# Softmax division on ScalarE and GpSimd, its small constant stored beside the sums, and a schedule recomputed with shifts as users of the shared port

## The chip, the cores and the metric

The kernel runs on one core of one Trainium2 chip. The metric is the device time of one execution in microseconds; of several runs the median counts. A core has five engines that run side by side, each through its own list of instructions in order: TensorE (PE; its weight loads are shown apart as PEld), VectorE (DVE), ScalarE (ACT), GpSimd (POOL) and SyncE (SP), which here only issues DMAs.

## The reference

An attention over 4 batches, 8 heads, 768 positions and 64 dimensions, then a two-layer feed-forward with GELU on the 3072 x 512 result.

```python
scores = scale * np.matmul(q, k.transpose(0, 1, 3, 2))
keep = is_global | is_local              # 8 global columns, a causal window of 96
scores = scores + bias                   # -slope * distance, a slope for each head
scores = np.where(keep, scores, -1000000000.0)
scores = scores - np.max(scores, axis=-1, keepdims=True)
a = np.exp(scores)
a = a / (np.sum(a, axis=-1, keepdims=True) + 1e-09)
attn = np.matmul(a, v)
x = attn.transpose(0, 2, 1, 3).reshape(3072, 512)
h = x @ w_in                             # 512 -> 2048
g = 0.5 * h * (1.0 + erf(h / sqrt(2)))
out = g @ w_out                          # 2048 -> 512
```

The line that the change is about is the division `a / (sum + 1e-09)`.

## The kernel before, in words

The program has two parts. The first one does the attention, the first quarter of the feed-forward and the preparation of all weights. The second one does the other three quarters of the feed-forward by a scheme with fewer products (seven for eight), from weights that the first part wrote to memory.

First part: the tokens are cut into 12 chunks of 256 (three for each batch), and each chunk has 4 pairs of heads. Each piece of work is an operation with a letter, listed in `first_part`:

- `l` (SP) loads the queries, keys and values of one pair. `S` (PE, line 214) makes its scores, two banks of PSUM for each pair, one for each head. A head has two blocks of 128 rows; each is 256 columns wide, or one of them 128 in a batch's first chunk.
- `R` (DVE, line 231) adds the penalties, keeps the maximum (`nmax`) and writes the head's tile `pn`. `E` (ACT, line 244) takes the exponential in place, and its accumulator writes the row sum into `nsum`.
- `U` (DVE, lines 249 and 250) adds 1e-9 to the four sums of a pair and takes the reciprocal, both in place in `nsum`. There are 48 `U`.
- `N` (line 256) multiplies `pn` by the reciprocal, two instructions for each of the 96 heads, on DVE or on GpSimd.
- `T` (PE, line 266) transposes, `C` (ACT or DVE, through the helper `copy`, line 179) copies the result to SBUF as `pt`, and `A` (PE, line 287) multiplies by the values.
- `X` and `Y` split the result in a high and a low part, `W` (POOL, line 307) adds them up and `Z` writes them out. `m` (PE, lines 421 and 433), `G` (ACT, GELU), `K` (DVE, `gl`) and `n` (PE, line 457) are the feed-forward's first quarter, and `O` (ACT or DVE) copies its sums to the tile `o`.
- Weights arrive as 64-bit words. `D` (ACT line 322 or POOL line 320) scales the low word, `F` (DVE, line 327) shifts the high word, `j` (DVE, line 332) joins, `J` (POOL or DVE, line 337) adds the low bits. `H`, `L`, `Q`, `h`, `o` and `B` split, sum and store them (`wst`, `sums`).

The second part (from line 536 on) runs products `p` and `m2` on PE in a fixed order, with sums, GELUs and splits on DVE and ACT between.

The order on every engine is decided by `schedule`, which plays a list of costs through once while the program is built. An operation has one or several engines with a cost for each; it goes to the engine on which it would be done first, moved by a number from `BIAS`. Operations that the planner takes to use one port into SBUF, which DVE and GpSimd share, are marked `port=True`, and it lets no marked DVE operation overlap a GpSimd operation. Before the change `F` and `N` are not marked on DVE. `CAP` says how many PSUM banks a kind may hold (`ks` is for scores), and `DEC` gives due times for the weights' preparation. What the planner found is kept: each engine runs its instructions in that order and waits for what they need.

Of the kernel before, what the change touches and what calls it, by code (L numbers as in the profile page):

```python
# [64 lines left out]
def slope(h):  # L65
# [4 lines left out]
SUMS2 = {1: (0, 0), 2: (0, 1), 7: (1, 0), 5: (1, 1), 4: (2, 0), 3: (2, 1), 6: (3, 0)}  # L70
SLOTS = {"k": 8, "nat": 6, "pn": 10, "pt": 10, "x": 3, "xw": 1, "ws": 4, "wa": 4, "wst": 2, "sums": 1, "g": 3, "o": 2,
         "hc1": 2, "hc6": 2, "hc5": 2, "gb0": 5, "gb1": 7, "gx": 2}
CAP = {"ks": 4, "kt": 3, "ka": 2, "kh": 2, "ko": 2, "kb": 4}
KEEP = {"ks": 1, "kt": 1, "ka": 1, "kh": 1, "ko": 3}
SOON, SLACK, WINDOW, LAT, LAT0, IDLE = 0.0, 0.1, 12, 0.262, .05, 28.189
BIAS = {("POOL", "N"): -0.593, ("POOL", "J"): -1.118, ("POOL", "L"): -0.258, ("POOL", "Q"): -0.723, ("POOL", "o"): 0.179, ("POOL", "D"): 0.298,
        ("ACT", "C"): -0.106, ("ACT", "X"): -0.272, ("ACT", "D"): -0.2, ("ACT", "H"): -0.564, ("ACT", "O"): -0.35}
BIAS_FRONT = {("POOL", "N"): -0.845, ("POOL", "J"): -0.4, ("POOL", "L"): -0.546, ("POOL", "Q"): -0.511, ("POOL", "o"): -0.181, ("POOL", "D"): -0.51,
              ("ACT", "C"): -0.331, ("ACT", "X"): -0.4, ("ACT", "D"): -0.96, ("ACT", "H"): -0.4, ("ACT", "O"): -0.845}
FRONT = 26.926  # L80
SPLIT, CHECK = 1, 8
W2_AFTER = {(3, 1): ("p", 1, 1), (4, 0): ("p", 1, 4), (4, 1): ("p", 2, 4), (5, 0): ("p", 3, 4), (5, 1): ("p", 4, 4)}
BN = ("b", "z")
COUNTS = (3, 6, 4, 2, 6, 3)
# [5 lines left out]
KEYS = {  # L90
    "S": lambda g: g + -1.513,
    "T": lambda g: g + 0.835,
    "A": lambda g: g + 1.916,
    "m": lambda c, s: 4 * c + 6.0 + 0.626 * s,
    "n": lambda c, s: 4 * c + 8.948 + 0.4 * s,
}

# [11 lines left out]
class Fast:  # L109
# [29 lines left out]
    def consts(self):  # L139
        nc, const = self.nc, self.const  # L140
        pen = self.pen = const.tile([P, 3 * P], BF16, name="pen")
        self.nmax = const.tile([P, NCH * NP, 4], F32, name="nmax")
        self.nsum = const.tile([P, NCH * NP, 4], F32, name="nsum")
        self.pens = self.pnp.tile([P, H, 3 * P], BF16, name="pens")
        self.wand = const.tile([P, 256], I32, name="wand")
        self.ident = const.tile([P, P], F32, name="ident")
        ta = self.es.tile([P, 4, 256], F32, name="ta")
        tb = self.es.tile([P, 2, 256], F32, name="tb")
        irel, icol = tb[:, 0].bitcast(I32), tb[:, 1, 0:P].bitcast(I32)
        rel, col, near, base = ta[:, 0], ta[:, 1, 0:P], ta[:, 2], ta[:, 3]  # L150
# [88 lines left out]
    def exps(self, c, h):  # L239
        nn = self.t["pn", (c, h)]  # L240
        for j, w in enumerate(self.widths(c)):
            i = h % 2 * 2 + j
            k = c * NP + h // 2
            self.nc.scalar.activation(out=nn[:, j, :w], in_=nn[:, j, :w], func=AF.Exp, bias=self.nmax[:, k, i:i + 1],  # L244
                                      scale=-1.0, accum_out=self.nsum[:, k, i:i + 1])

    def inverse(self, c, p):
        su = self.nsum[:, c * NP + p]
        self.nc.vector.tensor_scalar(out=su, in0=su, scalar1=1e-9, scalar2=None, op0=ALU.add)
        self.nc.vector.reciprocal(out=su, in_=su)  # L250

    def scale(self, e, c, h):
        nn = self.t["pn", (c, h)]
        for j, w in enumerate(self.widths(c)):
            i = h % 2 * 2 + j
            self.eng(e).tensor_scalar(out=nn[:, j, :w], in0=nn[:, j, :w], scalar1=self.nsum[:, c * NP + h // 2, i:i + 1],  # L256
                                      scalar2=0.0, op0=ALU.mult, op1=ALU.add)

    def parts(self, c):
        return [(0, 0), (1, 0), (1, 1)] if c % CPB == 0 else [(0, 0), (0, 1), (1, 0), (1, 1)]  # L260
# [395 lines left out]
    def first_part(self):  # L656
# [4 lines left out]
        for c in range(NCH):  # L661
            f = c % CPB == 0
            for p in range(NP):
# [6 lines left out]
                for h in (2 * p, 2 * p + 1):  # L670
                    op(("R", c, h), ("DVE", (.7, .56)[f]), lambda e, c=c, h=h: self.reduce(c, h), [("S", c, p), ("P", h)],
                       alloc=[("pn", (c, h))], free=[("k", ("s", c, h))])
                    op(("E", c, h), ("ACT", (.986, .88)[f]), lambda e, c=c, h=h: self.exps(c, h), [("R", c, h)])
                op(("U", c, p), ("DVE", .29), lambda e, c=c, p=p: self.inverse(c, p), [("E", c, 2 * p), ("E", c, 2 * p + 1)])
                for h in (2 * p, 2 * p + 1):
                    op(("N", c, h), [("DVE", (.53, .47)[f]), ("POOL", (.95, .85)[f])], lambda e, c=c, h=h: self.scale(e, c, h),
                       [("U", c, p)])
                    op(("T", c, h), ("PE", (.42, .31)[f]), lambda e, c=c, h=h: self.flip(c, h), [("N", c, h)],
                       alloc=[("k", ("t", c, h))], free=[("pn", (c, h))], key=lag["T"](g) + .001 * (h % 2))
                    op(("C", c, h), [("ACT", (.49, .39)[f]), ("DVE", (.6, .47)[f])],  # L680
# [16 lines left out]
                if p % 2:  # L697
                    need = [("Y", c, p - 1), ("Y", c, p)] if c < 2 else [("Y", c, p // 2)]
                    need.append(self.at("W", c, 0))
                    op(("W", c, p // 2), ("POOL", 1.29), lambda e, c=c, p=p: self.x_whole(c, p // 2), need,  # L700
                       alloc=[("xw", c)] if p == 1 else [], free=[("x", c)], due=(("A", c, p), 12.0))
            op(("Z", c), ("SP", ISSUE), lambda e, c=c: self.spill(c), [("W", c, 0), ("W", c, 1)], free=[("xw", c)], kb=512, due=(("A", c, 3), 16.0))
        for s in range(NST):
            for i in range(4):
                a = s < NA
                op(("w", s, i), ("SP", ISSUE), lambda e, s=s, i=i: self.load_words(s, i), alloc=[("ws", (s, i))], kb=512)
                op(("D", s, i), [("ACT", .565), ("POOL", 1.0)], lambda e, s=s, i=i: self.low_bits(e, s, i), [("w", s, i)])
                op(("F", s, i), ("DVE", .34), lambda e, s=s, i=i: self.shift_words(s, i), [("w", s, i)], alloc=[("wa", (s, i))])
                op(("j", s, i), ("DVE", .6), lambda e, s=s, i=i: self.join_words(s, i), [("F", s, i)], port=True)
                op(("J", s, i), [("POOL", 1.27), ("DVE", .6)], lambda e, s=s, i=i: self.round_word(e, s, i),  # L710
                   [("D", s, i), ("j", s, i)], free=[("ws", (s, i))], port=True)
# [696 lines left out]
```

## Time and profile before

| | us |
|---|---|
| median of 3 runs | 700.58 |
| lowest and highest of them | 699.02 to 701.56 |
| the profiled execution, its own time | 697.96 |
| its span from the first to the last instruction | 696.1 |

| engine | busy us | share of the span |
|---|---|---|
| PE | 658.2 | 95% |
| PE's weight loads | 600.7 | 86% |
| DVE | 582.1 | 84% |
| ACT | 421.7 | 61% |
| POOL | 195.8 | 28% |

The shares are averages over two parts with different loads. The first part ends at about 319 us of the span, when the first product of line 536 starts on PE, and nearly all of GpSimd's work lies ahead of that point. So a change in the first part has to be read from the windows and the waits of that part.

### The profile page before, as it was taken

The numbers are of one execution on the slowest core, as the hardware profiler recorded it, in microseconds if no ns is written. First come the engines' busy times: TensorE is split into PE (matmuls) and PEld (weight loads), VectorE is DVE, ScalarE is ACT, GpSimd is POOL, SyncE is SP. The second block draws the span as 40 slices with busy tenths as digits, with TensorE's granted clock in tenths as the row PEclk, the third lists the DMA queues.
The fourth block names the chain that finished last, engine by engine and source line by source line (L and its number), as shares of the span: only waits on it lengthen the run. The fifth ranks groups of instructions, "written<-read, shape, count | busy, mean of one in ns | idle before, by whom it ended". The sixth has DMA issues, their size and how long they took to land. (4 is left out here: it accounts for less than half of the span.)

```text
span 696.1 us, 14892 instructions
## 1 busy us (share of the span) xinstructions
PE 658.2 (95%) x5363; PEld 600.7 (86%) x5363; DVE 582.1 (84%) x1624; ACT 421.7 (61%) x1071; POOL 195.8 (28%) x230
## 2 busy tenths in 40 slices
PE   8789899789989899999999999999999999999996
PEld 6567678677778688789999999999999999999995
DVE  7999999999999898764659878967987897797775
ACT  5798786876867687735555446445544644554450
POOL 4668476766768555320000000000000000000002
PEclk9999999999999899999999999999999999999999
DMA  8666487879686768996999698878979887885501
GB/s 294 234 235 203 171 294 293 330 245 333 262 332 235 247 247 307 351 401 236 345 414 411 226 337 287 313 289 310 349 235 333 275 338 279 298 313 188 202 2 65
DMA packets 48897, 192.41 MB, mean 276 GB/s; under 512 B 5552, under 2 KB 6064, under 8 KB 41904
## 3 DMA queue, kind: packets, MB, share of 16 engines
q1 hardware_dynamic: 48384, 191.12, 74.8%
q8 instruction: 44, 0.72, 0.4%
q14 instruction: 37, 0.30, 0.1%
q10 hardware_dynamic: 432, 0.26, 0.1%
HBM read 150.47 MB, written 40.89 MB: 275 GB/s over the span
## 5 line engine op out<-in xcount | busy, mean ns | idle before, releaser
L594 PE MATMUL k<-w,go 128*128 128x256 f32 x1512 | 194.2, 282 | 1.0 <-DVE hc L546 0.7
L594 PEld LDWEIGHTS k<-w,go 128*128 128x128 f32 x1512 | 185.5, 189 | 2.2 <-DVE hc L546 0.9
L244 ACT ACTIVATE pn<-pn,nmax 128x256 f32<-128x256 f32 (+1 forms) x192 | 92.2, 483 | 37.2 <-DVE nmax L231 36.9
L536 PE MATMUL k<-xch,w1a 128*128 128x256 f32 x576 | 110.4, 284 | 0.0
L603 POOL TENSOR_TENSOR part<-part,r 128x256 f32<-128x256 f32 x1 | 0.7, 743 | 370.5 <-DVE r L603 370.5
L536 PEld LDWEIGHTS k<-xch,w1a 128*128 128x128 f32 x576 | 92.6, 191 | 0.3
L536 PE MATMUL k<-xch,w1b 128*128 128x256 f32 x432 | 91.6, 282 | 0.8 <-ACT hc L542 0.5
L536 PE MATMUL k<-xcl,w1a 128*128 128x256 f32 x288 | 81.4, 283 | 0.0
L546 DVE TENSOR_TENSOR hc<-hc,k 128x256 f32<-128x256 f32 x108 | 45.0, 417 | 42.1 <-ACT hc L542 32.2
L542 ACT COPY hc<-k 128x256 f32<-128x256 f32 x108 | 39.7, 368 | 62.9 <-PE k L536 62.9
L536 PEld LDWEIGHTS k<-xch,w1b 128*128 128x128 f32 x432 | 72.8, 190 | 1.3 <-ACT hc L542 0.7
L578 ACT CAST go<-gb 128x384 fp32r<-128x384 f32 x72 | 37.0, 513 | 55.4 <-PE k L594 54.9
L231 DVE CUSTOM_DVE_ANT_0 pn<-k,pens 128x256 f32<-128x256 f32 (+1 forms) x192 | 66.7, 393 | 4.1 <-PE k L214 2.8
L266 PE MATMUL k<-ident,pn 128*128 128x128 f32 x352 | 51.4, 284 | 19.1 <-DVE nmax L231 10.2
L554 ACT ACTIVATE gb<-hc 128x256 f32<-128x256 f32 x108 | 45.2, 419 | 39.6 <-DVE hc L546 38.4
L266 PEld LDWEIGHTS k<-ident,pn 128*128 128x128 f32 x352 | 38.9, 143 | 32.6 <-issue 13.2
L256 POOL TENSOR_SCALAR pn<-pn,nsum 128x256 f32<-128x256 f32 (+1 forms) x86 | 46.5, 553 | 53.6 <-DVE nsum L250 35.0
L536 PE MATMUL k<-xcl,w1b 128*128 128x256 f32 x216 | 60.9, 282 | 0.0
L214 PE MATMUL k<-nat 64*128 64x256 f32 (+1 forms) x384 | 54.1, 399 | 5.6 <-DVE pt L179 2.6
L182 DVE TENSOR_TENSOR go<-gb,go 128x384 fp32r<-128x384 f32 x72 | 40.0, 555 | 19.4 <-ACT go L578 19.0
L256 DVE TENSOR_SCALAR pn<-pn,nsum 128x256 f32<-128x256 f32 (+1 forms) x106 | 55.7, 571 | 0.4
L536 PEld LDWEIGHTS k<-xcl,w1a 128*128 128x128 f32 x288 | 55.1, 191 | 0.0
(123 smaller groups left out, 1505.1 us busy)
## 6 DMA issues: line engine op xcount, KB each, us to landing
w1a<-w1d SPq DMA_DIRECT2D x36, 1024.0 KB, 7.4
w1b<-w1d SPq DMA_DIRECT2D x36, 768.0 KB, 4.8
nat<-qkv SPq DMA_DIRECT2D x32, 640.0 KB, 5.1
ws<-w SPq DMA_DIRECT2D x32, 512.0 KB, 5.1
c<-w SPq DMA_DIRECT2D x64, 256.0 KB, 5.1
w1d<-wst SPq DMA_DIRECT2D x6, 1792.0 KB, 7.7
w2d<-wst SPq DMA_DIRECT2D x6, 1792.0 KB, 6.8
nat<-qkv SPq DMA_DIRECT2D x16, 384.0 KB, 4.7
```

Of the source, the lines that this page charges most:

```text
L182: self.eng(e).tensor_tensor(out=out, in0=in_, in1=hi.bitcast(F32), op=ALU.subtract)
L214: self.nc.tensor.matmul(sp[hh][:, j, :w], lhsT=qq[hr, j * P:(j + 1) * P], rhs=kt[hr, 0 if first else j, :w], start=True, stop=True)
L231: self.nc.vector.tensor_tensor_reduce(out=nn[:, j, :w], in0=sp[:, j, :w], in1=pen, scale=-0.125, scalar=3e38, op0=ALU.add, op1=ALU.min, ac ...
L244: self.nc.scalar.activation(out=nn[:, j, :w], in_=nn[:, j, :w], func=AF.Exp, bias=self.nmax[:, k, i:i + 1], scale=-1.0, accum_out=self.nsu ...
L256: self.eng(e).tensor_scalar(out=nn[:, j, :w], in0=nn[:, j, :w], scalar1=self.nsum[:, c * NP + h // 2, i:i + 1], scalar2=0.0, op0=ALU.mult, ...
L266: self.nc.tensor.transpose(tp[:, i, :], nn[:, j, a * P:(a + 1) * P], self.ident)
L536: self.nc.tensor.matmul(out, lhsT=w[:, i, d * P:(d + 1) * P], rhs=y[:, d, :], start=bool(new) and n == 0, stop=n == 5, skip_group_check=no ...
L542: self.nc.scalar.copy(x, self.t["k", ("x", u)])
L546: self.nc.vector.tensor_tensor(out=x, in0=x, in1=self.t["k", (bank, u)], op=ALU.add)
L554: self.nc.scalar.activation(out=out, in_=src, func=AF.Gelu)
L578: self.nc.scalar.copy(o[:, 0, dst], src)
L594: self.nc.tensor.matmul(out[k], lhsT=o[:, i, a], rhs=w[:, b, j], start=s == 0 and n == 0 and k in (1, 4, 5, 6), stop=s == NB - 1 and n == ...
```

## The change

1. `U` no longer adds 1e-9 by an instruction of its own form. `nsum` is now an array with two numbers for each sum: the first is what the exponential's accumulator writes, the second is 1e-9, stored once at the start. `U` sums each two with a `tensor_reduce` and writes the reciprocals to a tile of their own, `ninv`. Both tiles have room for three chunks, used in turn.
2. `N` may also run on ScalarE, as an activation `Copy` whose scale is the reciprocal.
3. `N` and `F` are marked as users of the shared port when they are on DVE.
4. The planner's costs and table of numbers are new: `CAP["ks"]` falls from 4 to 2, `U` is .32 for .29, `N` on GpSimd 1.0 for .95, `W` 1.35 for 1.29, `D` on GpSimd 1.67 for 1.0, and `BIAS`, `KEYS` and `DEC` have other numbers. So the order on every engine in the first part is another one. In the second part the order on PE is the same row for row.

```diff
-CAP = {"ks": 4, "kt": 3, "ka": 2, "kh": 2, "ko": 2, "kb": 4}
+CAP = {"ks": 2, "kt": 3, "ka": 2, "kh": 2, "ko": 2, "kb": 4}
...
-DEC = {(s, i): 57.774 + 7.541 * (4 * (s - NA) + i) for s in range(NA, NST) for i in range(4)}
+DEC = {(s, i): 57.774 + 7.137 * (4 * (s - NA) + i) for s in range(NA, NST) for i in range(4)}
...
-        self.nsum = const.tile([P, NCH * NP, 4], F32, name="nsum")
+        self.nsum = const.tile([P, RING, NP, 4, 2], F32, name="nsum")
+        self.ninv = const.tile([P, RING, NP, 4], F32, name="ninv")
...
+        nc.vector.memset(self.nsum[:, :, :, :, 1:2], 1e-9)
...
-                                      scale=-1.0, accum_out=self.nsum[:, k, i:i + 1])
+                                      scale=-1.0, accum_out=self.nsum[:, c % RING, h // 2, i, 0:1])
 
     def inverse(self, c, p):
-        su = self.nsum[:, c * NP + p]
-        self.nc.vector.tensor_scalar(out=su, in0=su, scalar1=1e-9, scalar2=None, op0=ALU.add)
-        self.nc.vector.reciprocal(out=su, in_=su)
+        ps = slice(p, p + UNITE)
+        to = self.ninv[:, c % RING, ps].rearrange("q p i -> q (p i)")
+        self.nc.vector.tensor_reduce(out=to, in_=self.nsum[:, c % RING, ps].rearrange("q p i n -> q (p i) n"),
+                                     axis=mybir.AxisListType.X, op=ALU.add)
+        self.nc.vector.reciprocal(out=to, in_=to)
 
     def scale(self, e, c, h):
...
-            self.eng(e).tensor_scalar(out=nn[:, j, :w], in0=nn[:, j, :w], scalar1=self.nsum[:, c * NP + h // 2, i:i + 1],
-                                      scalar2=0.0, op0=ALU.mult, op1=ALU.add)
+            by = self.ninv[:, c % RING, h // 2, i:i + 1]
+            if e == "ACT":
+                self.nc.scalar.activation(out=nn[:, j, :w], in_=nn[:, j, :w], func=AF.Copy, scale=by)
+                continue
+            self.eng(e).tensor_scalar(out=nn[:, j, :w], in0=nn[:, j, :w], scalar1=by, scalar2=0.0, op0=ALU.mult, op1=ALU.add)
...
-                    op(("N", c, h), [("DVE", (.53, .47)[f]), ("POOL", (.95, .85)[f])], lambda e, c=c, h=h: self.scale(e, c, h),
-                       [("U", c, p)])
+                    op(("N", c, h), [("DVE", (.53, .47)[f]), ("POOL", (1.0, .85)[f]), ("ACT", (.8, .71)[f])],
+                       lambda e, c=c, h=h: self.scale(e, c, h), [("U", c, p // UNITE)], port=True)
...
-                op(("D", s, i), [("ACT", .565), ("POOL", 1.0)], lambda e, s=s, i=i: self.low_bits(e, s, i), [("w", s, i)])
-                op(("F", s, i), ("DVE", .34), lambda e, s=s, i=i: self.shift_words(s, i), [("w", s, i)], alloc=[("wa", (s, i))])
+                op(("D", s, i), [("ACT", .565), ("POOL", 1.67)], lambda e, s=s, i=i: self.low_bits(e, s, i), [("w", s, i)])
+                op(("F", s, i), ("DVE", .34), lambda e, s=s, i=i: self.shift_words(s, i), [("w", s, i)], alloc=[("wa", (s, i))],
+                   port=True)
```

Counted over the whole program, these instructions stand on another engine than before, or are gone:

| operation | before | now |
|---|---|---|
| `N`, 128x256 | DVE 90, POOL 70 | ACT 102, POOL 58 |
| `N`, 128x128 | DVE 16, POOL 16 | ACT 20, POOL 12 |
| `C` (copies to `pt`), 128x512 | ACT 34, DVE 30 | ACT 19, DVE 45 |
| `C` (copies to `pt`), 128x384 | ACT 20, DVE 12 | ACT 11, DVE 21 |
| `O` (copies to `o`), 128x512 | ACT 23, DVE 1 | ACT 1, DVE 23 |
| `D` (low words), 128x512 | ACT 18, POOL 14 | ACT 25, POOL 7 |
| `J` (adding low bits), 128x512 | POOL 29, DVE 3 | POOL 31, DVE 1 |
| loads of an activation table in the first part | ACT 24 | ACT 22 |

The first place is DVE around the 26th of the 48 inverses, in chunk 6 (the first of the third batch). Before, with `xl` as the low part of an attention output and `pn` as a head's exponentials:

```order
L249 TENSOR_SCALAR nsum<-nsum 128x4
L250 RECIPROCAL nsum<-nsum 128x4
L182 TENSOR_TENSOR xl_1889<-k_2071,xh_1888 128x512
L231 ISA pn_2158,nmax<-k_2091,pens 128x128
L231 ISA nmax 128x1
L231 ISA pn_2158,nmax<-k_2091,pens 128x256
L231 ISA nmax 128x1
L256 TENSOR_SCALAR pn_2100<-pn_2100,nsum 128x128
L256 TENSOR_SCALAR pn_2100<-pn_2100,nsum 128x256
```

DVE around the same inverse, now (`pt` is a transposed head, `o` a sum of the feed-forward):

```order
L252 TENSOR_REDUCE ninv<-nsum 128x4
L254 RECIPROCAL ninv<-ninv 128x4
L181 COPY pt_2152<-k_2133 128x384
L184 TENSOR_TENSOR xl_1926<-k_2053,xh_1925 128x512
L181 COPY o_2166<-k_2072 128x512
L181 COPY pt_2177<-k_2160 128x384
L181 COPY o_2187<-k_2087 128x512
```

The two `N` instructions of line 256 are gone from DVE, and copies of `pt` and of `o` have come.

The second place is ACT behind the GELUs of chunk 6 (five more chunks' GELUs follow), where the table for the exponential is loaded again. Before:

```order
L244 ACT_TABLE_LOAD
L244 ACTIVATE pn_2386,nsum<-pn_2386,nmax 128x256 x2
L244 ACTIVATE pn_2414,nsum<-pn_2414,nmax 128x256 x2
L179 COPY pt_2460<-k_2408 128x512
L179 CAST xh_2220<-k_2389 128x512
L179 CAST wst_2305<-sums_2306 128x2x256 x2
L244 ACTIVATE pn_2444,nsum<-pn_2444,nmax 128x256 x2
L179 COPY o_2494<-k_2437 128x512
```

ACT behind the GELU of the same place, now:

```order
L246 ACT_TABLE_LOAD
L246 ACTIVATE pn_2347,nsum<-pn_2347,nmax 128x256 x2
L246 ACTIVATE pn_2356,nsum<-pn_2356,nmax 128x256 x2
L181 CAST wst_2319<-wa_2261 128x2x2x128
L181 CAST wst_2319<-sums_2320 128x2x256
L246 ACTIVATE pn_2409,nsum<-pn_2409,nmax 128x256 x2
L262 ACTIVATE pn_2356<-pn_2356,ninv 128x256 x2
L181 CAST wst_2319<-sums_2320 128x2x256
L246 ACTIVATE pn_2417,nsum<-pn_2417,nmax 128x256 x2
L181 CAST xh_2253<-k_2376 128x512
```

The `N` of `pn_2356` (line 262) stands three instructions behind its own exponential, one head's exponential among them; it needs the reciprocal that DVE makes in between. The copies of `pt` and `o` have left this piece of ACT's list.

## Rows read from the trace of the kernel before

**Rows 1.** The windows view: busy us (instructions) of each engine in three stretches.
```profile
0.00:240.00 240.00, 210.43 (x1679) 168.30 (x1680) 226.76 (x655) 178.56 (x482) 159.97 (x184) 0.97 0.73 265
240.00:318.00 78.00, 78.00 (x629) 65.66 (x628) 62.89 (x177) 55.01 (x143) 32.34 (x41) 1.00 0.86 323
318.00:696.00 378.00, 369.80 (x3059) 366.77 (x3057) 292.49 (x794) 188.12 (x449) 3.55 (x5) 1.00 0.75 274
```

**Rows 2.** PE's longest waits from 0 to 240 us: total us, times, longest.
```profile
PE k L266 <- DVE nmax L231: 10.2, 5, 3.5
PE k L266 <- DVE gl L182: 3.5, 1, 3.5
PE k L266 <- DVE pt L179: 3.3, 2, 2.8
```

**Rows 3.** Lines by form, division and inverse: busy us, mean ns | idle before, releaser.
```profile
L256 DVE TENSOR_SCALAR pn<-pn,nsum 128x256 f32<-128x256 f32 x90 | 49.5, 589 | 0.4
L256 DVE TENSOR_SCALAR pn<-pn,nsum 128x128 f32<-128x128 f32 x16 | 7.6, 473 | 0.1
L256 POOL TENSOR_SCALAR pn<-pn,nsum 128x256 f32<-128x256 f32 x70 | 39.7, 576 | 36.2 <-DVE nsum L250 23.9 <-ACT pn L244 5.7 <-PE k L266 2.3
L256 POOL TENSOR_SCALAR pn<-pn,nsum 128x128 f32<-128x128 f32 x16 | 7.2, 452 | 17.4 <-DVE nsum L250 11.1 <-ACT wst L179 2.6 <-DVE nmax L231 1.3
L249 DVE TENSOR_SCALAR nsum<-nsum 128x4 f32<-128x4 f32 x48 | 15.0, 313 | 5.3 <-ACT pn L244 5.3
L250 DVE RECIPROCAL nsum<-nsum 128x4 f32<-128x4 f32 x48 | 8.5, 178 | 1.7
```

**Rows 4.** The timeline at 154 us: start, us, instruction; a division beside two GpSimd additions.
```profile
154.06 1.29 POOL L337 TENSOR_TENSOR wa<-wa,ws 128x512 int32<-128x512 int32 x1
154.17 2.57 DVE L256 TENSOR_SCALAR pn<-pn,nsum 128x128 f32<-128x128 f32 x2
155.32 1.27 POOL L182 TENSOR_TENSOR wst<-sums,wst 128x512 fp32r<-128x512 f32 x1
```

**Rows 5.** Single lines' instructions: ns of the shortest/median/longest, first and last start.
```profile
L256 DVE TENSOR_SCALAR pn<-pn,nsum x106: 274/490/1401, 12.2 to 298.7; 128x256 f32<-128x256 f32 x90, 128x128 f32<-128x128 f32 x16
L249 DVE TENSOR_SCALAR nsum<-nsum x48: 153/162/1259, 11.3 to 298.0; 128x4 f32<-128x4 f32 x48
L327 DVE TENSOR_SCALAR wa<-ws x32: 396/470/1539, 15.0 to 247.4; 128x512 int32<-128x512 int32 x32
```

**Rows 6.** Lines by form: what moves to DVE or away from ACT and POOL.
```profile
L179 DVE COPY pt<-k 128x512 f32<-128x512 f32 x30 | 19.6, 680 | 4.3 <-PE k L266 4.2
L179 DVE COPY pt<-k 128x384 f32<-128x384 f32 x12 | 6.2, 548 | 1.1 <-PE k L266 1.1
L179 ACT COPY pt<-k 128x512 f32<-128x512 f32 x34 | 18.9, 584 | 12.7 <-PE k L266 10.5 <-PE k L287 1.9
L179 ACT COPY pt<-k 128x384 f32<-128x384 f32 x20 | 8.9, 478 | 5.4 <-PE k L266 3.0 <-PE k L287 2.3
L327 DVE TENSOR_SCALAR wa<-ws 128x512 int32<-128x512 int32 x32 | 22.2, 714 | 0.0
L320 POOL TENSOR_SCALAR ws<-ws 128x512 int32<-128x512 uint32 x14 | 23.8, 1697 | 1.2
```

**Rows 7.** Lines by form on ACT: the nearest rows to a division there, and a table load.
```profile
L244 ACT ACTIVATE pn<-pn,nmax 128x256 f32<-128x256 f32 x160 | 79.5, 500 | 18.3 <-DVE nmax L231 18.2
L542 ACT COPY hc<-k 128x256 f32<-128x256 f32 x108 | 39.7, 368 | 62.9 <-PE k L536 62.9
L244 ACT ACT_TABLE_LOAD x12 | 15.4, 1283 | 1.4 <-PEq L1392 1.2
```

**Rows 8.** The windows view of line 256 alone: busy us (instructions) of DVE, then POOL.
```profile
0.00:240.00 240.00, 46.31 (x84) 34.77 (x64) 0.97 0.73 265
```

**Rows 9.** The timeline at 153.7 us: the score matmuls of one pair on PE.
```profile
153.71 0.93 PE L214 MATMUL k<-nat 64*128 64x128 f32 x8 [1.20 <-DVE pt L179]
```

**Rows 10.** DVE's waits for score matmuls from 0 to 240 us.
```profile
DVE pn L231 <- PE k L214: 1.5, 3, 0.9
```

More of the change, by code (lines that the diff above doesn't have):

```diff
@@ L72 @@
          "hc1": 2, "hc6": 2, "hc5": 2, "gb0": 5, "gb1": 7, "gx": 2}
-CAP = {"ks": 4, "kt": 3, "ka": 2, "kh": 2, "ko": 2, "kb": 4}
+CAP = {"ks": 2, "kt": 3, "ka": 2, "kh": 2, "ko": 2, "kb": 4}
 KEEP = {"ks": 1, "kt": 1, "ka": 1, "kh": 1, "ko": 3}
[L75 to L79, printed above, removed]
+SOON, SLACK, WINDOW, LAT, LAT0, IDLE = 0.0, 0.1, 12, 0.255, .05, 19.761
+BIAS = {("POOL", "N"): -0.649, ("POOL", "J"): -0.767, ("POOL", "L"): -0.258, ("POOL", "Q"): -0.723, ("POOL", "o"): 0.987, ("POOL", "D"): 0.298,
+        ("ACT", "C"): -0.32, ("ACT", "X"): -0.532, ("ACT", "D"): -0.2, ("ACT", "H"): -0.564, ("ACT", "O"): 0.236, ("ACT", "N"): -0.47}
+BIAS_FRONT = {("POOL", "N"): -0.845, ("POOL", "J"): -0.4, ("POOL", "L"): -0.546, ("POOL", "Q"): -0.235, ("POOL", "o"): -0.181, ("POOL", "D"): -0.51,
+              ("ACT", "C"): -0.331, ("ACT", "X"): -1.028, ("ACT", "D"): -0.917, ("ACT", "H"): -0.35, ("ACT", "O"): -0.845, ("ACT", "N"): -0.4}
 FRONT = 26.926
-SPLIT, CHECK = 1, 8
+SPLIT, CHECK, UNITE, RING = 1, 8, 1, 3
 W2_AFTER = {(3, 1): ("p", 1, 1), (4, 0): ("p", 1, 4), (4, 1): ("p", 2, 4), (5, 0): ("p", 3, 4), (5, 1): ("p", 4, 4)}
@@ L88 @@
 FREE = (5.6, 4.0, 6.1, 6.2, .8)
-DEC = {(s, i): 57.774 + 7.541 * (4 * (s - NA) + i) for s in range(NA, NST) for i in range(4)}
+DEC = {(s, i): 57.774 + 7.137 * (4 * (s - NA) + i) for s in range(NA, NST) for i in range(4)}
 KEYS = {
[L91 to L94, printed above, removed]
+    "S": lambda g: g + -1.051,
+    "T": lambda g: g + 0.62,
+    "A": lambda g: g + 2.296,
+    "m": lambda c, s: 4 * c + 5.994 + 0.626 * s,
     "n": lambda c, s: 4 * c + 8.948 + 0.4 * s,
@@ L673, in first_part @@
                     op(("E", c, h), ("ACT", (.986, .88)[f]), lambda e, c=c, h=h: self.exps(c, h), [("R", c, h)])
-                op(("U", c, p), ("DVE", .29), lambda e, c=c, p=p: self.inverse(c, p), [("E", c, 2 * p), ("E", c, 2 * p + 1)])
+                if p % UNITE == UNITE - 1:
+                    q = p - UNITE + 1
+                    op(("U", c, p // UNITE), ("DVE", .32), lambda e, c=c, q=q: self.inverse(c, q),
+                       [("E", c, h) for h in range(2 * q, 2 * p + 2)])
                 for h in (2 * p, 2 * p + 1):
-                    op(("N", c, h), [("DVE", (.53, .47)[f]), ("POOL", (.95, .85)[f])], lambda e, c=c, h=h: self.scale(e, c, h),
-                       [("U", c, p)])
+                    op(("N", c, h), [("DVE", (.53, .47)[f]), ("POOL", (1.0, .85)[f]), ("ACT", (.8, .71)[f])],
+                       lambda e, c=c, h=h: self.scale(e, c, h), [("U", c, p // UNITE)], port=True)
                     op(("T", c, h), ("PE", (.42, .31)[f]), lambda e, c=c, h=h: self.flip(c, h), [("N", c, h)],
@@ L699, in first_part @@
                     need.append(self.at("W", c, 0))
-                    op(("W", c, p // 2), ("POOL", 1.29), lambda e, c=c, p=p: self.x_whole(c, p // 2), need,
+                    op(("W", c, p // 2), ("POOL", 1.35), lambda e, c=c, p=p: self.x_whole(c, p // 2), need,
                        alloc=[("xw", c)] if p == 1 else [], free=[("x", c)], due=(("A", c, p), 12.0))
```

## The prediction

> **What bounds the kernel now.** I read the page first for the shares of the engines, then the windows view, then the waits of PE, then the lines of the operations that the change touches, and last one stretch of the timeline.
>
> The windows view cuts the span into three [rows 1]. From 318 us on PE is busy 369.8 of 378 us: the second part is PE's, and its order is the same before and now, so I look for no change there. From 240 to 318 us PE is busy 78.0 of 78.0 us, still on the first part. Only from 0 to 240 us does PE have gaps: 240 - 210.4 = 29.6 us. In that stretch DVE is busy 226.8 us, or 94.5%, and ACT and POOL 178.6 and 160.0. The waits say the same: the three longest groups of PE's waits there, 17.0 of the 29.6 us, are all ended by DVE [rows 2]. So the first 240 us are bound by DVE, and 29.6 us is about the most that any relief of it can bring (the granted clock is 0.97 there, which adds little).
>
> How much of DVE's time is work and how much is being held up? The timeline at 154 us shows it [rows 4]: two divisions, together 2.57 us, that end only behind two GpSimd additions of 1.29 and 1.27 us. The shortest division takes 274 ns [rows 5]; the mean of the wide ones is 589 [rows 3]. About half of DVE's 57 us of division is being held up by GpSimd. The same spread shows in line 249 (153 at the shortest, 313 in the mean) and in the shift of line 327 (396 and 714) [rows 3, 5, 6].
>
> **The change part by part.** All sums are for the first 240 us, which hold 46.3 + 34.8 = 81.1 [rows 8] of the 104.0 us of all divisions [rows 3], or 0.78; I use that share for what is counted over the whole program.
>
> *Divisions leave DVE.* All 106 go, and with them the 46.3 us of [rows 8].
>
> *The 1e-9.* The trace has no `tensor_reduce` of this size beside GpSimd. If it is held up like the addition it replaces it costs 0.313 us and gains nothing; at the addition's shortest, 0.153, it gains 48 x 0.160 = 7.7 us. I take 0.178, the mean of the reciprocal right behind it, which works on the same four numbers [rows 3]: 48 x 0.135 = 6.5, and 0.78 of that is 5.1 us. The constant's store is one instruction at the start, and reading it costs nothing of its own, as it lies inside the same operand.
>
> The Trainium skill has a rule on this, in "SBUF — State Buffer", section "Who interferes with whom": a `tensor_reduce` on this chip never contends with GpSimd, while a `tensor_scalar` can. By it the new form would stay near its shortest. The spread of line 249 agrees with its second half [rows 3, 5]; no run so far shows the first half. By the rule the sum would be 7.7 us and without it 0.
>
> *Shifts marked as port users.* 32 shifts lose at most 714 - 396 = 318 ns each [rows 5, 6], 10.2 us, if the planner always keeps them clear of GpSimd; at the least nothing, or a loss of as much if DVE now waits empty where it was held up before. The plan and the chip don't run in step, so I take half of the gain, 5.1 us, all before 247 us [rows 5].
>
> *Copies come to DVE.* 15 of `pt` at 0.680 and 9 at 0.548 are 15.1 us; 22 of `o` have the wide ones' shape and cost 15.0 [rows 6]. Together 30.1, and 0.78 of it is 23.5 us. Moves of one or two instructions (casts, low parts) stay under 2 us either way and are left out.
>
> DVE's sum: -46.3 - 5.1 - 5.1 + 23.5 = -33.0 us, so 226.8 becomes 193.8.
>
> *ACT.* It gets 122 divisions. No row shows an activation `Copy` with a scale for each row; the nearest are the exponential of the same shape with an accumulator, 500 ns, and a plain copy from PSUM, 368 [rows 7]. I take the middle, 0.434, and count the 20 narrow ones alike: 52.9 us (44.9 to 61.0). It gives away 15 + 22 wide copies at 0.584 and 9 narrow ones at 0.478, 25.9 us, and gets 7 passes over low words, at 0.584 each for their width, 4.1 us [rows 6]. That is +31.1, and 0.78 of it is 24.3. Two table loads at 1.283 us go [rows 7], both in the early chunks: -2.6. So ACT goes from 178.6 to 200.3 us, with 194 and 207 as ends.
>
> *POOL.* It loses 12 wide and 4 narrow divisions (8.7 us) and 7 passes at 1.697 (11.9), and gets 2 additions at 1.29 (2.6) [rows 3, 4, 6]: -18.0, times 0.78 -14.0, so 146 us.
>
> *PE* has the same instructions, 210.4 us, and is now the largest.
>
> *The end.* DVE as the bound ran 94.5% dense. If PE runs as dense, the work of the first 240 us takes 210.4 / 0.945 = 222.6 us, 17.4 less. If nothing comes of it PE stays at 210.4 / 240 = 87.7%. ACT at 200 and DVE at 194 us lie close under PE, and every head crosses all three (scores, maximum, exponential, sums, division, transpose, copy), so I take a little less than the upper end, 93.5%: 225 us, a gain of 15. The stretches behind it stay as they are but start earlier. From the profiled execution's own 697.96 us this gives 683.0. The runs' median is 2.6 us above that execution, so I forecast 685.5 us.
>
> **The rivals.**
>
> *PE closes nearly all its gaps.* Three quarters of them or more go, a gain of 22 to 29 us, and the time is 672 to 679. For it: the waits shown for PE end with DVE [rows 2], and DVE loses 33 us against 29.6 of gaps. Against it: the first pairs have nothing to overlap with, and the two next engines are within 16 us of PE.
>
> *Two score banks where there were four.* The scores of a pair can now start only when both reductions of the pair before have read theirs; so DVE can come to stand idle while PE makes the next scores, 0.93 us a pair [rows 9]. With all 47 handovers bare it costs 43.7 us, 34 in the stretch, and eats the whole relief of DVE. For it: with four banks DVE already waited 1.5 us for scores [rows 10]. Against it: in the new order at least three other DVE instructions stand between the reductions of two pairs in 44 of 47 places. With a quarter of them bare, 8.5 us, the gain is 6.5 and the time 694.
>
> *ACT stands in front of the division.* A division at the head of ACT's list waits for DVE's reciprocal, and behind it wait the exponentials of later heads, for which DVE, PE and everything else wait. GpSimd, which has this place before, stood 36.2 + 17.4 = 53.6 us ahead of its 43 heads, 1.25 us each; 35.0 us of that, 0.81 each, ended with the reciprocal [rows 3]. 61 heads now go to ACT, 48 of them in the stretch. With 0.81 us each ACT needs 200.3 + 39 = 239 us and nothing is gained; with 1.25 it needs 260 and the time is 697.96 + 20 + 2.6 = 721. It decides from (240 - 200.3) / 48 = 0.83 us a head. Against it: GpSimd is busy only two thirds of the stretch and comes early to what it waits for; ACT comes later, and in the new order other ACT work stands between a head's exponential and its division. The Trainium skill speaks for this side, in "ScalarE: Activation LUTs", section "Rules for kernel authors": plain multiplications go to VectorE. An undisturbed division on DVE bears it out, with 274 ns [rows 5]; its mean here, 589, does not [rows 3].
>
> *Stalls only change place.* The joins, low parts and shifts on DVE still meet GpSimd, the transposes come as late as before, and the time stays within 699 to 702. That instructions move is certain from the order; that the stalls go is not.
>
> **How the numbers follow.** The forecast, a gain of 7 to 22 us or 678 to 694, has 0.61. PE with hardly a gap has 0.14, the banks 0.12, ACT in front 0.10, stalls that change place 0.03. 0.3% is 2.1 us, about what a measurement of this kernel can tell from no change. Faster by more: 0.61 + 0.14 + 0.09 of the banks' case = 0.84. Within it: 0.03 + 0.02 = 0.05. Slower: 0.10 + 0.01 = 0.11. The range, 672 to 699 us, holds the forecast, nearly all of PE's and most of the banks' case, and leaves out ACT in front.
>
> **What would show each step.** The first product of line 543 (536 before) should start near 304 us of the span, not 319, and the distance from there to the end should stay at 377. Up to there DVE should be busy about 33 us less and ACT about 85% of the time. The wide division on ACT should take 0.37 to 0.50 us, the `tensor_reduce` 0.15 to 0.18 with no long ones among them, the shift's mean should fall towards 0.4 to 0.55. PE's waits should still end with DVE most often, but add up to half as much. ACT's waits for the reciprocal above 0.8 us a head would show the third rival, DVE's waits for scores above 10 us in total the second. The forecast is wrong if the first product starts after 312 us or before 297.

## The result and the profile after

The changed kernel takes 668.68 us (668.56 to 668.93, 4 runs) against 700.75 for the kernel before on the same chip: a ratio of 0.9546, 95% interval 0.9528 to 0.9564, or 32.1 us less. I forecast 685.5, with 672 to 699 as the range. The sign was right; the gain was twice the forecast, and the time lies just below the range. The two traces differ by less, 696.1 - 666.9 = 29.2 us, because the traced execution of the kernel before was one of its quickest (697.96 us).

The windows view of the changed kernel, cut where the first product of line 543 starts. The columns are the stretch, its length, the busy us (instructions) of PE, PE's weight loads, DVE, ACT and POOL, PE's granted clock, the share of DMA and GB/s:

```profile
0.00:288.90 288.90, 282.57 (x2315) 231.19 (x2316) 252.23 (x773) 257.23 (x703) 171.10 (x203) 1.00 0.83 307
288.90:666.90 378.00, 368.36 (x3051) 365.33 (x3049) 293.41 (x795) 187.11 (x446) 3.56 (x5) 0.99 0.75 274
```

The same cut of the kernel before:

```profile
0.00:318.98 318.98, 289.41 (x2314) 234.94 (x2315) 290.63 (x832) 233.69 (x623) 192.30 (x225) 0.98 0.76 278
318.98:696.00 377.02, 368.82 (x3051) 365.79 (x3049) 291.51 (x793) 188.00 (x448) 3.55 (x5) 1.00 0.75 275
```

The second part takes 378.0 us for 377.0. The gain is all in the first part, 319.0 - 288.9 = 30.1 us, and splits in two: PE's gaps fall from 319.0 - 289.4 = 29.6 to 288.9 - 282.6 = 6.3 us, which is 23.3; and PE's own busy time, for the same matmuls, falls by 6.8.

PE's waits in the first part, longest first (total us, times, longest), now:

```profile
PE k L216 <- DVE nmax L233: 1.2, 3, 0.7
PE idle L239 <- DVE wz L1187: 1.2, 1, 1.2
PE k L273 <- DVE nmax L233: 1.0, 2, 0.6
PE k L464 <- DVE xl L184: 0.7, 1, 0.7
```

The transposes that stood 10.2 us before, up to 3.5 at a time [rows 2], stand 1.0 us. The lines of the operations that moved, by form (busy us, mean ns | idle before, releaser):

```profile
L262 ACT ACTIVATE pn<-pn,ninv 128x256 f32<-128x256 f32 x102 | 46.1, 499 | 8.4 <-DVE ninv L254 8.3
L264 POOL TENSOR_SCALAR pn<-pn,ninv 128x256 f32<-128x256 f32 x58 | 28.6, 504 | 38.5 <-DVE ninv L254 34.0 <-ACT ws L329 2.6 <-ACT pn L246 1.7
L334 DVE TENSOR_SCALAR wa<-ws 128x512 int32<-128x512 int32 x32 | 21.4, 671 | 0.0
L252 DVE TENSOR_REDUCE ninv<-nsum 128x4 f32<-128x8 f32 x48 | 7.3, 152 | 3.0 <-ACT pn L246 2.8
```

A wide division costs 499 ns on ACT, where it was 589 on DVE [rows 3]. The sum over the constant takes 152 ns where the addition took 313. The shift has hardly changed, 671 for 714 [rows 6].

Where PE's own 6.8 us went shows in three stretches of the kernel before, each a gap of PE and the stretch behind it (columns as above):

```profile
44.60:47.60 3.00, 0.18 (x5) 0.06 (x2) 3.00 (x6) 2.93 (x7) 2.70 (x2) 1.00 0.69 213
47.60:52.00 4.40, 4.40 (x32) 3.14 (x32) 4.40 (x12) 3.04 (x7) 0.75 (x1) 0.66 0.68 218
68.40:72.10 3.70, 0.22 (x3) 0.05 (x2) 3.70 (x14) 1.36 (x5) 1.34 (x2) 1.00 0.38 130
72.10:76.00 3.90, 3.90 (x30) 3.32 (x32) 2.92 (x6) 2.71 (x6) 1.29 (x1) 0.61 0.01 4
227.50:231.00 3.50, 0.35 (x4) 0.15 (x2) 3.50 (x14) 0.98 (x5) 1.73 (x3) 0.85 0.42 172
231.00:236.50 5.50, 5.50 (x33) 4.19 (x34) 3.46 (x10) 4.99 (x12) 3.25 (x5) 0.50 0.98 345
```

In all three gaps DVE is busy throughout, and behind each the granted clock is 0.66, 0.61 and 0.50 in the mean, that is 1.2 instead of 2.4 GHz for most of it. The lost clock is 4.4 x 0.34 + 3.9 x 0.39 + 5.5 x 0.50 = 5.8 us of matmul time. The changed kernel has no such gap, and a clock of 1.00 in its first part.

### The profile page after: what moved, and what is told of

Read it like the earlier page. It is cut to its first block, busy times and chain, and to the rows that moved or that the text cites. A ratio compares the mean times of both kernels' runs of the same rounds, so it can differ in the third digit from the quotient of the medians.

```text
span 666.9 us, 14922 instructions
## 1 busy us (share of the span) xinstructions
PE 650.9 (98%) x5363; PEld 596.5 (89%) x5363; DVE 545.6 (82%) x1567; ACT 444.3 (67%) x1149; POOL 174.7 (26%) x208
## 5 line engine op out<-in xcount | busy, mean ns | idle before, releaser
L262 ACT ACTIVATE pn<-pn,ninv 128x256 f32<-128x256 f32 (+1 forms) x122 | 51.5, 482 | 9.9 <-DVE ninv L254 9.6
L184 DVE TENSOR_TENSOR go<-gb,go 128x384 fp32r<-128x384 f32 x72 | 39.9, 554 | 19.6 <-ACT go L585 19.1
L216 PE MATMUL k<-nat 64*128 64x256 f32 (+1 forms) x384 | 51.6, 386 | 1.3 <-DVE nmax L233 1.2
L428 PE MATMUL k<-xh,winh 128*128 128x256 f32 x176 | 52.4, 298 | 0.0
L344 POOL TENSOR_TENSOR wa<-wa,ws 128x512 int32<-128x512 int32 x31 | 43.7, 1414 | 30.0 <-DVE wa L339 15.6
```

Of the source, the lines that this page charges most:

```text
L184: self.eng(e).tensor_tensor(out=out, in0=in_, in1=hi.bitcast(F32), op=ALU.subtract)
L216: self.nc.tensor.matmul(sp[hh][:, j, :w], lhsT=qq[hr, j * P:(j + 1) * P], rhs=kt[hr, 0 if first else j, :w], start=True, stop=True)
L344: self.eng(e).tensor_tensor(out=a, in0=a, in1=self.t["ws", (s, i)][:, :, 0], op=ALU.add)
L428: nc.tensor.matmul(hp[:, f, :], lhsT=w[:, d, f * P:(f + 1) * P], rhs=x[:, d, :], start=n == 0, stop=n == 3 * NP - 1)
```

## The experiments

Two theories stood against each other. The relief theory: the first part was held by DVE, and what it is rid of comes back as time, wherever the work goes. The plan theory: the new numbers and marks bring the plan in step with the chip, and which engine divides matters little. All times below are medians, the ratios are to the kernel before on the same chip, with the 95% interval.

**e1, e2: one part of the change in the old order.** e1 keeps the old order row for row and only runs DVE's divisions on ACT:

```diff
-            o.fn(self.on[i])
+            e = self.on[i]
+            o.fn("ACT" if o.name[0] == "N" and e == "DVE" else e)
```

> The kernel before, its order kept row for row; only the 106 division instructions that stood on VectorE run on ScalarE, at the places that the old plan gave them. Relief theory (the first part was held by VectorE's 290.6 us, 55.7 of them division): VectorE falls to about 235 us of the first part, ScalarE rises from 234 to about 284, the first product starts 12 to 22 us earlier, time 679 to 689. Plan theory (the gain of 32 us comes from a plan that is in step with the chip, whatever engine divides): nothing is replanned, ScalarE gets work that the plan does not know, time 697 to 712.

682.91 us, ratio 0.9738 (0.9711 to 0.9764): 18.1 us faster without any replanning. PE's waits in its first part now end mostly with ACT; the two longest (total us, times, longest):

```profile
PE k L270 <- ACT pt L179: 3.5, 4, 0.9
PE k L270 <- ACT pn L257: 3.0, 4, 1.1
```

e2 keeps order and engines and only sums over the stored constant:

```diff
-        self.nc.vector.tensor_scalar(out=su, in0=su, scalar1=1e-9, scalar2=None, op0=ALU.add)
+        self.nc.vector.tensor_reduce(out=to, in_=self.nsum[:, c * NP + p], axis=mybir.AxisListType.X, op=ALU.add)
```

> The kernel before with one part of the change alone: the 1e-9 is added by a sum over a stored constant. Order and engines as before. The 48 instructions should take 0.152 us each, as in the changed kernel, for 0.313: 7.7 us less on VectorE. Relief theory: a us of VectorE in the first 240 us is worth most of a us, 3 to 7 us faster, time 694 to 698. Plan theory: below 1.5 us, time 699 to 701.

695.31 us, ratio 0.9922 (0.9900 to 0.9945): 5.7 us faster. Both hold to the relief theory. The windows of the first part, e1 and then e2:

```profile
0.00:302.90 302.90, 283.77 (x2314) 230.72 (x2315) 237.08 (x726) 270.30 (x729) 196.98 (x225) 1.00 0.80 293
```

```profile
0.00:315.00 315.00, 291.18 (x2315) 237.67 (x2316) 284.14 (x833) 232.95 (x623) 191.73 (x225) 0.97 0.77 282
```

With 6.5 us less of DVE the first part of e2 is 4.0 us shorter; with 53.6 less, and 36.6 more of ACT, that of e1 is 16.1. So the relief comes back, but not us for us: in e1 PE's gaps still are 302.9 - 283.8 = 19.1 us, of 29.6.

**e3, e11: the new order with the division back on DVE.** e3 is the mirror of e1:

```diff
+            o.fn("DVE" if o.name[0] == "N" and e == "ACT" else e)
```

> The changed kernel, its order kept; only the 122 division instructions of ScalarE run on VectorE, at the same places. Relief theory: VectorE gets 33 us (0.27 each, if GpSimd never holds one up) to 65 us (0.53, the old mean) on top of 252, so it is the bound again with 285 to 317 us: 10 to 35 us slower than 668.7, time 679 to 704, with long instructions among the divisions. Plan theory: the order is the good one, within 5 us, 668 to 674.

702.62 us, ratio 1.0032 (1.0012 to 1.0052): the whole gain is gone, though order, marks and numbers are the new ones. DVE is busy 296.1 us again in the first part (windows view), and a wide division takes 573 ns:

```profile
0.00:320.70 320.70, 291.26 (x2314) 233.40 (x2315) 296.07 (x895) 213.50 (x581) 171.65 (x203) 0.99 0.75 277
```

Its division by lines and form (busy us, mean ns | idle before):

```profile
L264 DVE TENSOR_SCALAR pn<-pn,ninv 128x256 f32<-128x256 f32 x102 | 55.2, 573 | 0.1
```

e11 also gives the copies to `pt` and `o` back to ACT (`elif o.name[0] in "OC" and e == "DVE": e = "ACT"`), so that DVE has about the changed kernel's load again.

> The changed kernel's order with engines exchanged in place: the 122 divisions of ScalarE on VectorE, and all copies to pt and o that VectorE made on ScalarE. VectorE gives 57 us of copies and gets 122 divisions: 33 us at 0.27, 65 at 0.53. If what counts is the sum of VectorE's work: 228 us of it undisturbed, 260 when held up as before, so 668 to 678. If it counts that divisions on VectorE are held up by GpSimd and come late, wherever the sum ends: 680 to 695.

687.13 us, ratio 0.9823 (0.9797 to 0.9848). DVE is busy 259.8 us in the first part, 7.6 more than in the changed kernel, but the first part is 17.5 us longer. Its divisions take 574 ns, and PE's longest wait is now for them:

```profile
PE k L273 <- DVE pn L264: 4.4, 7, 1.1
PE k L273 <- DVE nmax L233: 3.3, 3, 1.9
```

So the sum of DVE's work is not all. A division that is held up comes late to the transpose behind it as well (in e11 they take 270 to 1471 ns), but that is only a part: PE's gaps grow by 13.0 us to 19.3, of which 4.4 are these waits. The copies were moved too, and what they cost on ACT was not tried by itself.

**e4, e5, e6, e7: numbers, marks, banks.** e4 is the new code with all old numbers and four score banks.

> The changed code with the planner's old numbers (BIAS, KEYS, DEC, the four score banks, the old costs of D, W and N on GpSimd). The planner now puts no division on VectorE, 76 on ScalarE and 116 on GpSimd. Relief theory: VectorE is relieved all the same, two thirds or more of the 32 us stay, time 668 to 680. Plan theory: without the new numbers at most a third stays, time 689 to 703.

672.73 us, ratio 0.9593 (0.9567 to 0.9619). 28 of the 32 us stay; the new numbers are worth 3 to 4 (3.3 by the ratios). Its first part:

```profile
0.00:291.40 291.40, 283.23 (x2314) 232.65 (x2315) 238.13 (x753) 253.12 (x680) 201.89 (x248) 0.99 0.80 297
```

PE's gaps are 8.2 us here, with old numbers but in a recomputed order, where e1 has 19.1.

e5 adds only `port=True` to `N` and `F` in the kernel before.

> The kernel before with only the marks: division and shift count as users of the port when they are on VectorE. ScalarE may not divide, all numbers are old. The planner then sends all 192 divisions to GpSimd. Relief theory in its wide form (any engine with room will do): VectorE loses 55.7 us, GpSimd goes from 192 to about 250 us of a first part of 300, time 670 to 686. Rival, ScalarE is needed (GpSimd at 0.55 us a division comes too late, and by its longer hours it holds up more of VectorE's two-input work): 687 to 702.

688.35 us, ratio 0.9833 (0.9805 to 0.9862): past the relief theory's bounds and within the rival's. GpSimd is busy 233.4 of 303.2 us, at 618 ns a wide division. The first part still is 15.8 us shorter. But early in the second part, from 324 us on, PE stands once for 3.9 us, and the clock falls behind it as it did in the kernel before (first PE's wait and that of ACT ahead of it, then windows of PE alone; the columns behind PE are its clock, DMA and GB/s):

```profile
PE k L594 <- ACT go L578: 3.9, 1, 3.9
ACT go L578 <- DMA pd<-o: 3.7, 1, 3.7
```

```profile
303.20:323.20 20.00, 18.80 (x130) 1.00 0.96 359
323.20:343.20 20.00, 15.93 (x106) 0.83 0.88 352
324.00:328.00 4.00, 0.18 (x1) 0.97 1.04 415
328.00:332.00 4.00, 3.86 (x17) 0.50 1.01 428
```

e6 takes both marks out of the changed kernel.

> The changed kernel without the two marks, its other numbers kept: the planner puts 44 of the 192 divisions back on VectorE, 86 on ScalarE, 62 on GpSimd. Relief theory: 44 x 0.27 to 0.57 us, less 15 copies that leave VectorE, so 2 to 15 us more of it at 252 of 289 us: 671 to 685. Rival (the marks do nothing for the chip): 667 to 670.

682.53 us, ratio 0.9752 (0.9724 to 0.9780), within the relief theory's bounds: without the marks 44 divisions go back to DVE (613 ns a wide one) and 14 us of the gain are gone. The marks change only the plan, so this run shows what another plan costs, not an effect of theirs on the chip. For the shift itself the mark brings nothing that shows: it takes 589 ns here, 671 with it.

e7 gives the changed kernel four score banks (`CAP["ks"]` 4).

> The changed kernel with four PSUM banks for scores where it has two, replanned with its numbers. If two banks cost something as I feared (VectorE waits for scores: 6.9 us in the trace of the changed kernel), this is 1 to 5 us faster, 664 to 667.5. If the banks serve the transposes and sums better, 670 to 676. If it is neither, 667.5 to 670.

670.76 us, ratio 0.9587 (0.9559 to 0.9615): 2 us slower, hardly clear of the changed kernel's interval. DVE's waits for scores are 7.5 us in the first part with four banks and 6.9 with two. So the two banks cost nothing.

**e8, e9, e10, e13, e14, e15: what still limits.** These keep the new order. e8 adds the 1e-9 as before; e9 and e10 add small unread work to DVE or ACT; e14 and e15 are the same with a 64-byte tile; e13 has e9's 16-byte tile and no added work. (The cut below joins the added lines of all four; the tile is left out.)

```diff
+        for _ in range(2):                       # e9, e14: behind each inverse
+            self.nc.vector.tensor_reduce(out=self.spare, in_=..., axis=mybir.AxisListType.X, op=ALU.add)
+        if h % 4 != 3:                           # e10, e15: behind an exponential
+            self.nc.scalar.activation(out=self.spare, in_=self.ident[:, 0:4], func=AF.Copy)
```

> The changed kernel with the 1e-9 added as before (one tensor_scalar on the four sums), order kept row for row. The 48 instructions should take about 0.3 us again for 0.152, 7 us more on VectorE. If VectorE no longer decides (matmuls fill 98% of the first part): 0 to 2 us slower, 668.7 to 670.7. If it still decides us for us: 674 to 676.

> The changed kernel, order kept, with two more sums of four numbers on VectorE behind each of the 48 inverses, into a tile that nobody reads: 96 x 0.152 = 14.6 us of VectorE that never meet GpSimd. It asks how near VectorE still is to deciding. By the slope of the added constant (10.2 us of VectorE for 4.0 us of time): 5 to 7 us slower, 674 to 676. If the first part is TensorE's alone: 0 to 2 us, up to 670.7. If VectorE decides us for us: 681 to 684.

> The changed kernel, order kept, with 72 more small activations (128x4, into a tile that nobody reads) on ScalarE behind exponentials, about 0.2 us each, 14 us. ScalarE is busy 257 of 289 us there, VectorE 252. If ScalarE is as near to deciding as VectorE: 5 to 8 us slower, 674 to 677. If it has slack where VectorE has none: 0 to 3 us, 669 to 672.

> The changed kernel with a tile of 16 bytes a partition in front of all later tiles, set once and not used. e9 and e10 had such a tile, and there the second part, whose instructions are the changed kernel's, took 383.1 and 381.2 us for 378.0. If the shifted addresses are the cause: first product at 289 us as in the changed kernel, second part 381 to 383.5, time 671.5 to 674.5. If not, 668 to 669.5, and the added instructions work in another way.

> e9 with the unread tile 64 bytes wide for 16, all else alike: 14.6 us more of VectorE in the first part. If the addresses cost e9 its 5 us in the second part: 672 to 675, first product at 292 to 294 us. If the extra sums cost it all: 677 to 679.

> e10 with the unread tile 64 bytes wide for 16: 13.8 us more of ScalarE in the first part. ScalarE has slack: 668.5 to 670, first product before 291 us. ScalarE limits as VectorE does: 672 to 675.

| | median us | ratio | first part | second part |
|---|---|---|---|---|
| changed kernel | 668.68 | 0.9546 | 288.9 | 378.0 |
| e8, constant added | 672.70 | 0.9614 (0.9591 to 0.9638) | 294.2 | 376.7 |
| e9, DVE, 16 bytes | 677.95 | 0.9689 (0.9666 to 0.9712) | 293.2 | 383.1 |
| e10, ACT, 16 bytes | 672.91 | 0.9612 (0.9589 to 0.9634) | 289.7 | 381.2 |
| e13, 16 bytes alone | 670.75 | 0.9579 (0.9551 to 0.9607) | 288.6 | 380.1 |
| e14, DVE, 64 bytes | 673.89 | 0.9615 (0.9579 to 0.9651) | 293.0 | 379.7 |
| e15, ACT, 64 bytes | 667.95 | 0.9539 (0.9503 to 0.9576) | 289.1 | 377.1 |

Only e14 came out inside one of its cases; e15 is half a us below its slack case, e9 is 2 us above the slope's, and e8, e10 and e13 fell between theirs. e9 and e10 mixed two things. Their second parts are 3 to 5 us longer with unchanged instructions, and e13 shows 2 of that with the tile alone; so I go by the first parts and by e14 and e15. The first part of e14, then of e15:

```profile
0.00:293.00 293.00, 282.72 (x2314) 230.00 (x2315) 260.74 (x869) 258.18 (x703) 172.07 (x203) 1.00 0.82 303
```

```profile
0.00:289.10 289.10, 282.76 (x2314) 231.12 (x2315) 252.41 (x773) 262.94 (x775) 171.64 (x203) 1.00 0.83 307
```

By their own durations the added instructions are 14.0 us on DVE and 13.8 on ACT; busy time rises by less, as it counts an overlap of neighbours once. 8.5 us more busy time on DVE cost 4.1 us of first part; 5.7 more on ACT cost 0.2. e8 agrees: its additions take 392 ns in the mean again, DVE is busy 10.2 us more and the first part is 5.3 longer. So even now DVE has a say of about a half, and ACT none at the places tried, though it is the busier of the two. One thing is not separated: the sums of e14 stand between the reciprocal and the divisions that need it (ACT's waits there grow from 9.6 to 12.0 us), so part of their cost may lie in the place and not in the load.

**e12, e16: can it be bettered?** e12 makes one inverse for two pairs (`UNITE` 2), e16 sends ten of the copies to `o` to ACT by one number of `BIAS`.

> The changed kernel with one inverse for two pairs (24 instead of 48), replanned with its numbers: 24 x (0.152 + 0.178) = 7.9 us less on VectorE, but the first pair's division waits for the second pair's exponentials. By the slope of 0.4: 2 to 3 us faster, 665.5 to 667. If the later division costs as much: 668 to 672. If VectorE has no say any more: 668 to 669.

678.59 us, ratio 0.9691 (0.9673 to 0.9710): 10 us slower, with a first part of 298.3 us although DVE is busy 3.3 us less. That is beyond even the slowest case expected. Whether the later divisions or a plan without numbers of its own did that, this run doesn't tell.

> The changed kernel replanned with one number less by 0.2 (the leaning of ScalarE against the copies to o): 10 of the 23 copies to o go from VectorE to ScalarE, 3 copies to pt the other way. About 5 us less on VectorE, 4 more on ScalarE. If VectorE is the nearer to deciding and ScalarE has slack: 1 to 3 us faster, 665.5 to 667.5. If the new plan is off balance: 669 to 675.

670.91 us, ratio 0.9589 (0.9555 to 0.9623): 2 us slower, not clear of noise, with 3.5 us less of DVE: the case of a plan off balance. Nothing tried beats the changed kernel clear of noise.

## Why the prediction was wrong, point by point

*What bounds the kernel*: right. e1, e2 and e3 show that DVE held the first part, and the second part is as it was (377.0 and 378.0).

*How much of the division is being held up*: misread. The 274 ns that I set against the mean of the wide divisions belong to a narrow one. A stretch of the kernel before with wide ones alone (ns of the shortest/median/longest, first and last start):

```profile
L256 DVE TENSOR_SCALAR pn<-pn,nsum x21: 339/562/1391, 20.9 to 69.9; 128x256 f32<-128x256 f32 x21
```

With 339 ns for each wide and 274 for each narrow division 34.9 of the 57.1 us are work, so about two fifths are held up and not half. The sum doesn't use it; the 0.27 in what I expected of e3 and e11 should have been 0.34.

*DVE's sum*: near, in part by luck. Over the whole program, without the share of 0.78, my terms give -57.1 - 6.5 - 5.1 + 30.1 = -38.6 us; the first part lost 290.6 - 252.2 = 38.4. The inverse gained what the lower bound of its row said (152 ns; I took 178). The term for the shifts was mis-sized: 5.1 us forecast, 22.2 - 21.4 = 0.8 measured. That it doesn't show in the sum is luck: the work of lines 332 and 383 (339 and 390 now), which I had left alone, took 4.8 us less. The sum over the constant now, and the addition in the same place in e8 (as above):

```profile
L252 DVE TENSOR_REDUCE ninv<-nsum x48: 138/152/163, 11.4 to 268.0; 128x4 f32<-128x8 f32 x48
L251 DVE TENSOR_SCALAR ninv<-nsum x48: 153/171/1245, 11.5 to 273.3; 128x4 f32<-128x4 f32 x48
```

The Trainium skill states in "SBUF — State Buffer", section "Who interferes with whom", that a `tensor_reduce` never contends with GpSimd on this chip. The traces agree: with GpSimd busy 171.1 of 288.9 us the longest of the 48 sums takes 163 ns, while in e8 the `tensor_scalar` in the same place takes up to 1245.

*ACT*: the first part's busy time rose by 23.5 us; my terms over the whole program give 31.1 - 2.6 = 28.5. The divisions themselves take 46.1 + 7.9 = 54.0, 52.9 forecast. I added up mean times, and busy time counts an overlap of neighbours once, as e15 shows (13.8 us of added instructions, 5.7 of busy time). A wide division takes 499 ns, the upper of my two rows and not their middle. The Trainium skill has a rule that I passed over, in "ScalarE: Activation LUTs", section "What ACT_TABLE_LOAD costs": 186 ns + 0.833 ns an element, and about 93 ns for each operand that is a pointer. By it, an estimate, a wide division with its scale from a tile takes 186 + 93 + 213 = 492 ns. The trace agrees within 2%.

*The end*: this is the step that failed. I let PE run 93.5% dense, below the 94.5% that DVE had as the bound, because "ACT at 200 and DVE at 194 us lie close under PE". Here is the middle of the first part, in the changed kernel, the kernel before and e1:

```profile
60.00:240.00 180.00, 179.02 (x1480) 146.52 (x1482) 167.81 (x494) 173.69 (x470) 122.70 (x134) 1.00 0.85 315
60.00:240.00 180.00, 160.81 (x1287) 130.10 (x1287) 171.94 (x468) 135.08 (x355) 123.03 (x136) 0.97 0.74 270
60.00:240.00 180.00, 172.01 (x1407) 139.80 (x1408) 149.13 (x438) 170.18 (x459) 137.08 (x149) 1.00 0.80 294
```

PE is 99.5% busy now, with ACT at 96.5% and DVE at 93.2% beside it; before it was 89.3%. Two engines close under PE didn't hold it back, and small work added to ACT costs nothing (e15). But that holds for the recomputed order. In e1, the old order, DVE lost more than all of PE's gaps, and yet PE is 95.6% busy and waits mostly for ACT; its first product starts at 302.9 us, where I had 304 for the changed kernel. So my density comes near what moving the division within the old order gives. What it left out is that the planner arranges the other work around the move: the first part's gaps are 29.6 us before, 19.1 in e1, 8.2 in e4 (replanned with old numbers, with the constant's sum and the marks) and 6.3 in the changed kernel. That was the rival that I gave 0.14, "PE closes nearly all its gaps"; for two more reasons its 672 to 679 us were still too many.

*The clock*: the second miss. I wrote that the granted clock of 0.97 "adds little". 0.03 x 240 is 7 us, and PE's busy time fell by 6.8. So the 29.6 us of gaps were not the most that could come back: gaps and clock together were 36, of which 30.1 came.

*The step from the trace to the median*: the third. I added 2.6 us, as the median before lay that much above the profiled execution. The executions of the kernel before spread, and the slower ones show the lower clock: on one chip 697.43 us at 0.988 and 703.31 at 0.977. The changed kernel's four lie within 0.4 us, at 0.996 to 0.998, so the 2.6 us are gone too. Of the 16.8 us between forecast and result 8.3 are gaps (23.3 for 15.0), 6.8 PE's own time and 2.6 this step, less 1.0 by which the second part is longer.

*The rivals*: two score banks cost nothing (e7), and DVE's waits for scores stay under the 10 us that I had set as their sign. ACT in front of the division didn't come (total us, times, longest):

```profile
ACT pn L262 <- DVE ninv L254: 9.6, 18, 1.3
```

That is 0.16 us for each of the 61 heads, where I had the point of decision at 0.83.

*Which part of the change did it*: from e1, about 18 of the 32 us come from where the division runs alone. From e4 and the changed kernel, 3 to 4 from the new numbers. e2's 5.7 is the constant's share in the old order, and e8's 4 to 5 in the new one. The rest, some 5, lies in replanning around the moved work, which no run has by itself. These shares were taken from different starting points and needn't add up.

## What to carry to other kernels

When one engine ends nearly all the waits of the engine that must be dense, its relief can close nearly all of those gaps, and the density that the old bound had is no measure for the new one. But don't count the relief us for us: 53.6 us less of DVE closed 10.5 of 29.6 us of gaps as long as the order stayed (e1). Recompute the order around the moved work. A busy share alone doesn't tell which engine limits: over the first part ACT is busy 89% in e1 and in the changed kernel, and in the one it ends most of PE's waits, in the other none; a small load added to it shows the difference. Count with each long gap of TensorE, like the three of 3.0 to 3.7 us here, the slower stretch behind it. And compare an instruction's mean with the shortest of the same shape: 339 ns beside 589 for the wide division says that the work is being held up, and moving it can be worth more than its own cost.

## What the runs showed of the hardware that was not expected

A tile of 16 bytes a partition in front of the others goes with slower matmuls in the second part, whose instructions are the same. Its length alone doesn't show that: it is 380.1 us in e13, 383.1 and 381.2 in e9 and e10, but 376.7 to 379.2 among the runs without such a tile (e5 apart), and 379.7 and 377.1 with 64 bytes. PE's busy time does: 371.2, 371.6 and 371.4 us in the three with 16 bytes, 367.4 and 367.3 in the two with 64, and 368.1 to 368.9 in the changed kernel and its seven runs with the same tiles (e3, e4, e6, e7, e11, e12, e16). e8, whose `nsum` is half as large, has 367.0. The second parts of e13 and e15:

```profile
288.60:668.70 380.10, 371.18 (x3051) 368.16 (x3049) 293.63 (x795) 187.16 (x446) 3.55 (x5) 1.00 0.74 273
289.10:666.20 377.10, 367.32 (x3051) 364.13 (x3049) 293.56 (x795) 187.13 (x446) 3.55 (x5) 1.00 0.75 275
```

The count of matmuls is the same, and PE's gaps, the stretch less PE's busy time, are no larger in e13 than in the changed kernel (8.9 and 9.6 us), so the matmuls run a little longer, without a wait. That the shifted addresses do it is the nearest reading, but which tile it is was not tried, and why was not either.

In e5's second part a wait of 3.9 us is followed by 4 us at a granted clock of 0.50 and goes with a mean of 0.83 over 20 us; that part takes 385.7 us. PE waited for a cast of GELU results on ACT, and by the trace that cast had itself waited 3.7 us for a DMA (`pd`, written out from `o`), while the 16 DMA engines were busy throughout. Why only this run has it was not tried. A plan that is good to the end of the first part can still lose this way behind it.
